# The gradient of one MLP weight moved to GpSimd at the turn of an attention block's training step, and three stores moved to the sync engine's queue

## Chip, cores and metric

The kernel runs on one core of one Trainium2 chip. The metric is the device time of one execution in microseconds; lower is better. Each kernel is timed several times, and its median is compared.

## What is computed

One decode step (one token, one batch) of a conditioned block, forward and backward in one launch. `c` is the condition, `w_mod` turns it into six modulation vectors; attention runs over a cache of 8192 keys and values for each of 32 heads of 192; the mixer behind it has an MLP of width 1536.

```python
mod = (_silu(c) @ w_mod).reshape(c.shape[0], 6, 1, -1)     # sa, ca, ga, sb, cb, gb
h = _layernorm(x) * (1 + ca) + sa
# _A_ref: q = h @ wq; p = softmax(q k^T / sqrt(192)); o = p v; o @ wo
x = x + ga * _A_ref(h, A_k_cache, A_v_cache, A_wq, A_wo)
h = _layernorm(x) * (1 + cb) + sb
# _B_ref at sequence length 1: the shifted half is zero, so
#   h + gelu(_layernorm(h) @ w3) @ w4
x = x + gb * _B_ref(h, B_w1, B_w2, B_w3, B_w4)
_out, _vjp = jax.vjp(_f, A_x, A_k_cache, A_v_cache, A_wq, A_wo, B_w3, B_w4, c, w_mod)
_grads = _vjp(grad_out)
```

The outputs are the result and nine gradients. The two large ones are those of the caches, dK and dV, 32 x 8192 x 192 in bfloat16 each (100 MB each). For one token each weight's gradient is an outer product of two vectors. The one that the change is about is dW4, the gradient of `B_w4` (1536 x 640): column `g` (the gelu's output, 1536) times row `dbo` (grad_out * gb, 640).

## The kernel before

**Forward (lines 493 to 591).** A loop over heads, two stages deep. Each head loads K and V in two tiles of 128 x 32 x 192 (1536 KB), on the queue of the sync engine (SP); DVE multiplies K by the broadcast q, TensorE sums, DVE and ScalarE (ACT) make the softmax, and TensorE accumulates K and V weighted by it.

**Turn (lines 592 to 778).** The MLP's forward and the start of the backward pass, on columns of 5 or 12 elements per partition. It is a serial chain between DVE and TensorE: two layernorms, `u` (L710 to 715), the gelu's parts, `du_bf` (L730), `g_f` (L732) and `g_bf` (L734), then `dn2` (L738), `dhb`, `dx1` and `dao_bf` (L742 to 755), and from it `do_bf` of the first pair of heads and its broadcast `do_pb` (L1044 to 1050).

**Backward (lines 1053 to 1099).** A loop over i = 0 to 31 with heads in falling order (`HS`: 31, 30, ...). For each head: `bwd_mult` multiplies both V tiles in place by `do_pb` on DVE, and TensorE sums them; `bwd_dv` makes dV for the next head, 20 of 32 columns of a tile on ACT (L877) and 12 on DVE (`pairs_outer`, L854), and stores it; `bwd_ds` and `bwd_dk` make dS and dK on DVE, and store dK. The dV of the first head, `HS[0]` = 31, is made ahead of the loop: its first tile all on DVE and stored in two halves of 768 KB, its second tile split as usual and stored in one of 1536 KB.

**Buffers.** dK and dV tiles come from the pool `big` (5 buffers). V tiles of the backward pass go round in six buffers of the pools `fv` and `bv`; `ring_load` issues a load as soon as the program has passed the place where an older tile was used up, and the load waits on the queue for that. Output tiles of the weight gradients come from the pool `bso`, tag "so", 2 buffers.

**Queues.** All loads of K, V and the weights in the loops go out from SP. All stores go out from GpSimd (POOL): `st2 = nc.gpsimd` (L675). POOL does nothing else after the constants at the start but to issue loads of `B_w3` and `B_w4` near the end of the forward pass. Each queue is served in the program's order; the orders of TensorE, DVE and ACT are pinned to the program's order by hand (`pin_order`), those of SP and POOL are what the program gives.

**Side jobs.** The outer products of the weights are spread over the backward loop by three lists, J0, J1, J2. `dbo_bc` (dbo broadcast to all partitions, 128 x 640 bfloat16) is made in the forward pass (L308), `g_f` at the turn; dW4 is made in four jobs, `job_dw4(k)`, at i = 17 to 20, each with three products of 128 x 640 on ACT (`tsc` with k = 0, L913) and one store of 480 KB. dW3 follows at i = 21 to 25, on DVE. dWo has gone ahead, at i = 1 to 16, and dWq and dWmod run from i = 9 on with loads, products and stores of their own.

Of the kernel before, what the change touches and what calls it, by code (L numbers as in the profile page):

```python
# [9 lines left out]
BF16 = mybir.dt.bfloat16  # L10
ALU = mybir.AluOpType
# [9 lines left out]
def kernel(  # L21
# [26 lines left out]
    nc = tc.nc  # L48
# [16 lines left out]
    P = 128  # L65
    D = A_x.shape[-1]
# [9 lines left out]
    NFC = F // P  # L76
    NMC = NMOD // P
    HH = HQ // 2
# [15 lines left out]
    def bank(tag, bufs=1, name=None, n=512):  # L94
        return psum[0].tile([P, n], FP32, tag=tag, name=name or "ps_" + tag, bufs=bufs)
# [31 lines left out]
    def ccol(n, name, dtype=FP32):  # L127
        return const.tile([P, n], dtype, name=name)
# [23 lines left out]
    def ln_cols(x_c, pfx, fill=lambda k: None):  # L152
        s1 = ccol(1, pfx + "_s1")
        nc.vector.reduce_sum(out=s1, in_=x_c, axis=AX.X)
        m_ps = neg_means(s1, 1, pfx + "_m")
        fill(0)
        xc = ccol(NDC, pfx + "_xc")
        add(xc, x_c, m_ps.to_broadcast([P, NDC]))
        sq = ccol(NDC, pfx + "_sq")
        s2 = ccol(1, pfx + "_s2")  # L160
        nc.vector.tensor_tensor_reduce(out=sq, in0=xc, in1=xc, scale=1.0 / D, scalar=0.0, op0=ALU.mult, op1=ALU.add, accum_out=s2)
        v_ps = col_sums(s2, 1, pfx + "_v")
        std = ccol(1, pfx + "_std")
        nc.scalar.activation(out=std, in_=v_ps, func=ACT.Sqrt, bias=eps_c[:, 0:1], scale=1.0)
        rstd = ccol(1, pfx + "_rstd")
        nc.vector.reciprocal(out=rstd, in_=std)
        fill(1)
        nrm = ccol(NDC, pfx + "_n")
        nc.vector.tensor_scalar(out=nrm, in0=xc, scalar1=rstd[:, 0:1], scalar2=None, op0=ALU.mult)
        return nrm, rstd  # L170
# [25 lines left out]
    def dve_copy(out, in_):  # L196
        nc.vector.tensor_copy(out=out, in_=in_)
# [11 lines left out]
    dV_hd = [out_3[0, h].rearrange("(p j) d -> p j d", p=P) for h in range(HQ)]  # L209
# [14 lines left out]
    def big_tile(name):  # L224
        return big.tile([P, JH, DH], BF16, name=name, tag="big")
# [44 lines left out]
    n0_c, r0 = ln_cols(x0_c, "ln0")  # L270
# [37 lines left out]
    dbo_bc = const.tile([P, D], BF16, name="dbo_bc")  # L308
# [214 lines left out]
    for i in range(1, HQ + 2):  # L523
        if i == HQ + 1:
            nc.scalar.activation(out=warm, in_=eps_c, func=ACT.Sqrt)
        c, p, pp = 2 <= i < HQ, 0 <= i - 1 < HQ, 0 <= i - 2 < HQ
# [75 lines left out]
    def w3T_some(n):  # L602
        for g in range(w3T_next[0], min(w3T_next[0] + n, NFC * NDC // 4)):
            t_ps = bank("s", 2, "t_ps", SB[0])
            for k in range(4):
                f, i = divmod(4 * g + k, NDC)
                nc.tensor.matmul(t_ps[:, k * P : (k + 1) * P], lhsT=w3n(i, f * P, (f + 1) * P), rhs=ident_bf, start=True, stop=True)
            k, r = divmod(g, NBT)
            nc.scalar.copy(out=w3T_t[k][:, r * 512 : (r + 1) * 512], in_=t_ps[:, 0:512])
        w3T_next[0] += n  # L610
# [30 lines left out]
    bso = ctx.enter_context(tc.tile_pool(name="bso", bufs=2, reuse_waits="tile"))  # L641
    bsm = ctx.enter_context(tc.tile_pool(name="bsmall", bufs=2, reuse_waits="tile"))
    HS = list(range(HQ - 1, -1, -1))
# [31 lines left out]
    st2 = nc.gpsimd  # L675
# [22 lines left out]
    n1_c, r1 = ln_cols(x1_c, "ln1", lambda k: w3T_some(k + 1))  # L698
# [32 lines left out]
    g_f = ccol(NFC, "g_f")  # L731
    mul(g_f, u, sg)  # L732
    g_bf = ccol(NFC, "g_bf", BF16)
    dve_copy(g_bf, g_f)  # L734
    dn2_ps = bank("b")
    for i in range(NDC):
        for f in range(NFC):
# [115 lines left out]
    def pairs_outer(o, pairs, vec, n):  # L853
        nc.vector.tensor_tensor(  # L854
            out=o.rearrange("p j (d r) -> p j d r", r=2),
            in0=pairs[:, :, None, :].to_broadcast([P, n, NP2, 2]),
            in1=vec.rearrange("p (d r) -> p d r", r=2)[:, None, :, :].to_broadcast([P, n, NP2, 2]),
            op=ALU.mult)

    def vec_of(d, h):  # L860
        return d[h // 2][:, (h % 2) * DH : (h % 2 + 1) * DH]
# [10 lines left out]
    def bwd_dv(h, t, na=NAV // 2, parts=1):  # L872
        o = big_tile("dV")
        j0 = t * JH
        doh = vec_of(do_pb, h)
        for jj in range(na):
            nc.scalar.activation(out=o[:, jj, :], in_=doh, func=ACT.Copy, scale=bst[h]["PF"][:, j0 + jj : j0 + jj + 1])  # L877
        n = JH // parts
        for r0 in range(0, JH, n):
            r1 = r0 + n  # L880
            ra = max(r0, na)
            pairs_outer(o[:, ra:r1, :], bst[h]["P2h"][:, j0 + ra : j0 + r1, :], doh, r1 - ra)
            st2.dma_start(out=dV_hd[h][:, j0 + r0 : j0 + r1, :], in_=o[:, r0:r1, :])  # L883

    def bwd_ds(h):
        dP = bsm.tile([P, J], FP32, name="dP")
# [24 lines left out]
    def tsc(out, in_, col, k):  # L911
        if k % 2 == 0:
            nc.scalar.activation(out=out, in_=in_, func=ACT.Copy, scale=col)  # L913
        else:
            nc.vector.tensor_scalar(out=out, in0=in_, scalar1=col, scalar2=None, op0=ALU.mult)

    def job_dw4(k):
        o = bso.tile([P, 3, D], BF16, name="dw4", tag="so")
        for cc in range(3):
            tsc(o[:, cc, :], dbo_bc, g_f[:, 3 * k + cc : 3 * k + cc + 1], 0)  # L920
        st2.dma_start(out=out_7[3 * k * P : 3 * (k + 1) * P, :].rearrange("(c p) r -> p c r", p=P), in_=o)

    def job_dw3(i):
        o = bso.tile([P, F], BF16, name="dw3", tag="so")
        tsc(o, du_bc, n2_c[:, i : i + 1], 1)
        st2.dma_start(out=out_6[i * P : (i + 1) * P, :], in_=o)

    def job_dwo(hp):
        o = bso.tile([P, 3, D], BF16, name="dwo", tag="so")
        for cc in range(3):  # L930
            tsc(o[:, cc, :], dao_bc, o_col_f[:, 3 * hp + cc : 3 * hp + cc + 1], 0)
        st2.dma_start(out=out_5[3 * hp * P : 3 * (hp + 1) * P, :].rearrange("(c p) r -> p c r", p=P), in_=o)
# [60 lines left out]
    J0, J1, J2 = [{i: [] for i in range(HQ)} for _ in range(3)]  # L993
    for k in range(HH):
        J1[1 + k].append(lambda hp=PS[k]: job_dwo(hp))
    for k in range(4):
        J1[1 + HH + k].append(lambda k=k: job_dw4(k))
    for k in range(NDC):
        J1[5 + HH + k].append(lambda i=k: job_dw3(i))

    def add_outer(at, name, view, lo, n, col_bf, rows_f, dram, acc, first):
        J2[at].append(lambda: job_outer_load(name, view, lo, n))
# [16 lines left out]
    for b, ks in enumerate(BATCHES):  # L1019
        units = [(PS[k], cc) for k in ks for cc in range(3)]  # L1020
        i = 1 + 2 * b
# [29 lines left out]
    bcast_dao()  # L1051
    mid_mm()
    bwd_dv(HS[0], 0, 0, 2)
    c_first = fin_c(PS[0], 1)
    bwd_dv(HS[0], 1)
    AHEAD = 2 * NPH
    for i in range(HQ):
        h, nxt = HS[i], HS[i + 1] if i + 1 < HQ else None
# [12 lines left out]
        if nxt is not None:  # L1071
            bwd_pf(nxt)
            for t in range(2):
                bwd_dv(nxt, t)
# [56 lines left out]
```

## Time and profile before

| | before |
|---|---|
| median of 3 runs | 1399.75 us (1398.21 to 1404.72) |
| profiled execution | 1395.47 us |
| its span, first to last instruction | 1393.7 us |
| busy: TensorE, DVE, ACT, POOL | 855.0, 1079.2, 964.8, 115.3 us |
| moved by DMA | 570.81 MB, mean 410 GB/s |
| SP's queue (q1) | 339.16 MB, 59.2% of 16 engines' span |
| POOL's queue (q0) | 229.85 MB, 39.2% |
| mean granted TensorE clock | 0.780 |

The profile is of one execution; times within it are counted in us from the first instruction. "Busy" leaves out the sequencers' own work: on SP everything is of that kind, on POOL the issue of a DMA is counted. The DMA share is the mean busy share of the core's 16 DMA engines, so 1 means that no transfer can be added; it comes out a little over 1 where packets overlap.

### The profile page before, as it was taken

The numbers are of one execution on the slowest core, as the hardware profiler recorded it, in microseconds if no ns is written. First come the engines' busy times: TensorE is split into PE (matmuls) and PEld (weight loads), VectorE is DVE, ScalarE is ACT, GpSimd is POOL, SyncE is SP. The second block draws the span as 40 slices with busy tenths as digits, with TensorE's granted clock in tenths as the row PEclk, the third lists the DMA queues.
The fourth block names the chain that finished last, engine by engine and source line by source line (L and its number), as shares of the span: only waits on it lengthen the run. The fifth ranks groups of instructions, "written<-read, shape, count | busy, mean of one in ns | idle before, by whom it ended". The sixth has DMA issues, their size and how long they took to land. (4 is left out here: it accounts for less than half of the span.)

```text
span 1393.7 us, 28111 instructions
## 1 busy us (share of the span) xinstructions
PE 855.0 (61%) x11519; PEld 672.3 (48%) x11519; DVE 1079.2 (77%) x1276; ACT 964.8 (69%) x2633; POOL 115.3 (8%) x207
## 2 busy tenths in 40 slices
PE   3699999999999999737644552434332344423242
PEld 3577777777777777626534451223222233212231
DVE  3678888888887886699996984966768669768697
ACT  1578777787787787794787396567666766566672
POOL 0000000000000000011101110211112111111011
PEclk9799999999999999666666566666676666766666
DMA  9999999999999999599999999999999999999998
GB/s 392 416 417 411 411 419 412 416 416 418 401 419 409 410 418 387 210 388 425 426 426 426 426 428 427 428 427 426 427 419 425 427 424 413 427 420 420 398 382 365
DMA packets 71711, 570.81 MB, mean 410 GB/s; under 512 B 6878, under 2 KB 18398, under 8 KB 31134
## 3 DMA queue, kind: packets, MB, share of 16 engines
q1 hardware_dynamic: 46496, 339.16, 59.2%
q0 software_dynamic: 25056, 229.85, 39.2%
q8 instruction: 90, 1.47, 0.4%
q14 instruction: 39, 0.32, 0.1%
q10 hardware_dynamic: 30, 0.00, 0.0%
HBM read 343.08 MB, written 225.91 MB: 408 GB/s over the span
## 5 line engine op out<-in xcount | busy, mean ns | idle before, releaser
L877 ACT ACTIVATE dV<-do_pb,PF 128x192 bf16<-128x192 bf16 x1260 | 439.5, 440 | 90.1 <-DMA out_dram<-dK 67.7
L869 PE MATMUL dP_ps<-V_sb,ident_bf 128*128 128x256 bf16 x1536 | 231.4, 326 | 264.8 <-DVE V_sb L131 264.8
L385 ACT ACTIVATE EK<-K_sb,E_f 128x192 bf16<-128x192 bf16 x1024 | 364.7, 442 | 22.8 <-PE kb_ps L426 15.2
L869 PEld LDWEIGHTS <-ident_bf 128*128 128x128 bf16 x1536 | 179.1, 117 | 317.4 <-issue 182.8
L854 DVE TENSOR_TENSOR dK<-dS,q_pb 128x6144 bf16<-128x6144 bf16 (+1 forms) x67 | 213.2, 3212 | 46.6 <-DMA out_dram<-dK 43.3
L131 DVE TENSOR_TENSOR prod<-K_sb,q_pb 128x6144 bf16<-128x6144 bf16 x64 | 214.7, 3354 | 22.0 <-DMA K_sb<-in_A_k_cache_dram 18.8
L131 DVE TENSOR_TENSOR V_sb<-V_sb,do_pb 128x6144 bf16<-128x6144 bf16 x64 | 211.8, 3351 | 2.6 <-DMA V_sb<-in_A_v_cache_dram 2.6
L410 PE MATMUL ps_a<-EK,V_sb 128*128 128x193 bf16 x2048 | 203.0, 252 | 4.7 <-DMA V_sb<-in_A_v_cache_dram 3.9
L410 PEld LDWEIGHTS <-V_sb 128*128 128x128 bf16 x2048 | 176.3, 100 | 23.8 <-issue 17.7
L854 DVE TENSOR_TENSOR dV<-P2h,do_pb 128x2304 bf16<-128x2304 bf16 (+1 forms) x65 | 87.3, 1369 | 57.7 <-DMA out_dram<-dV 53.1
L393 DVE TENSOR_TENSOR EK<-K_sb,P2h 128x1536 bf16<-128x1536 bf16 x128 | 121.7, 951 | 0.0
L418 PE MATMUL ps_b<-EK,V_sb 128*64 128x193 bf16 x2048 | 110.7, 250 | 8.1 <-DVE MB_all L134 8.0
L353 PE MATMUL S_ps<-prod,ident_bf 64*64 64x256 bf16 x3072 | 98.8, 276 | 6.7 <-DVE prod L131 6.7
L418 PEld LDWEIGHTS <-V_sb 128*64 128x64 bf16 x2048 | 84.1, 109 | 29.1 <-issue 28.8
L353 PEld LDWEIGHTS <-ident_bf 64*64 64x64 bf16 x3072 | 81.5, 109 | 22.4 <-issue 21.8
L374 ACT ACTIVATE E_f<-sm_ps,negm 128x64 f32<-128x64 f32 x32 | 10.1, 315 | 103.0 <-DVE negm L372 103.0
L883 POOL DMA_DIRECT2D out_dram<-dV x65 | 34.9, 537 | 447.1 <-ACT dV L877 272.5
L426 PE MATMUL kb_ps<-EK,hot_bf 128*32 128x384 bf16 x1024 | 65.7, 334 | 0.5 <-DVE q_bf L298 0.5
L194 ACT CAST do_pb<-bc_ps 128x384 bf16<-128x384 f32 x16 | 7.5, 470 | 70.4 <-PE bc_ps L190 70.4
L955 PEld LDWEIGHTS <-ident_bf 128*128 128x128 bf16 x112 | 14.3, 127 | 86.7 <-issue 83.3
L898 POOL DMA_DIRECT2D out_dram<-dK x67 | 37.2, 556 | 179.5 <-DVE dK L854 141.7
L391 DVE CAST EK<-E_f 128x16 bf16<-128x16 f32 x128 | 25.4, 199 | 33.5 <-PE kb_ps L426 27.3
(249 smaller groups left out, 816.1 us busy)
## 6 DMA issues: line engine op xcount, KB each, us to landing
V_sb<-in_A_v_cache_dram SPq DMA_DIRECT2D x126, 1536.0 KB, 11.7
K_sb<-in_A_k_cache_dram SPq DMA_DIRECT2D x64, 1536.0 KB, 9.5
out_dram<-dV POOLq DMA_DIRECT2D x63, 1536.0 KB, 19.8
out_dram<-dK POOLq DMA_DIRECT2D x63, 1536.0 KB, 21.3
wq<-in_A_wq_dram SPq DMA_DIRECT2D x3, 2560.0 KB, 34.0
wo_t<-in_A_wo_dram SPq DMA_DIRECT2D x16, 480.0 KB, 9.7
out_dram<-dwo POOLq DMA_DIRECT2D x16, 480.0 KB, 20.5
wq<-in_A_wq_dram SPq DMA_DIRECT2D x4, 1920.0 KB, 30.7
```

Of the source, the lines that this page charges most:

```text
L131: nc.vector.tensor_tensor(out=out, in0=a, in1=b, op=ALU.mult)
L353: nc.tensor.matmul(st["S_ps"][c0 : c0 + 64, r, t * JH : (t + 1) * JH, :], lhsT=ident_bf[64 * r : 64 * r + 64, 64 * r : 64 * r + 64], rhs=p ...
L385: nc.scalar.activation(out=EK[:, jj, 0:DH], in_=K_st[h, t][:, r * JQ + jj, :], func=ACT.Copy, scale=st["E_f"][:, j : j + 1])
L393: nc.vector.tensor_tensor(out=EK[:, NA:JQ, 0:DH].rearrange("p j (d r) -> p j d r", r=2), in0=K_st[h, t][:, r * JQ + NA : (r + 1) * JQ, :]. ...
L410: nc.tensor.matmul(st["A_ps"][:, 0 : DH + 1], lhsT=V_sb[:, r * JQ + jj, a0:a1], rhs=EK[:, jj, 0 : DH + 1], start=(q == 0 and jj == 0), sto ...
L418: nc.tensor.matmul(st["B_ps"][g : g + 64, 0 : DH + 1], lhsT=V_sb[:, r * JQ + jj, b0:b1], rhs=EK[:, jj, 0 : DH + 1], start=(q == 0 and jj < ...
L426: nc.tensor.matmul(kb_ps[g : g + 32, 0 : 2 * DH], lhsT=hot_bf[:, HQ - 1 - h : 2 * HQ - 1 - h], rhs=EK[:, jj : jj + 2, 0:DH], start=(h == 0 ...
L854: nc.vector.tensor_tensor(out=o.rearrange("p j (d r) -> p j d r", r=2), in0=pairs[:, :, None, :].to_broadcast([P, n, NP2, 2]), in1=vec.rea ...
L869: nc.tensor.matmul(bst[h]["dP_ps"][:, t * JH : (t + 1) * JH, :], lhsT=ident_bf, rhs=V_sb[:, :, k * DS : (k + 1) * DS], start=(k == 0), sto ...
L877: nc.scalar.activation(out=o[:, jj, :], in_=doh, func=ACT.Copy, scale=bst[h]["PF"][:, j0 + jj : j0 + jj + 1])
L883: st2.dma_start(out=dV_hd[h][:, j0 + r0 : j0 + r1, :], in_=o[:, r0:r1, :])
L898: st2.dma_start(out=dK_hd[h][:, j0 : j0 + n, :], in_=o[:, r0 : r0 + n, :])
```

## The change

dW4's twelve products of 128 x 640 are taken from ACT and from the backward loop. They are written right behind `g_f` and `g_bf`, on POOL (`nc.gpsimd.tensor_scalar`, `dbo_bc` times a column of `g_f`), in four tiles of the same pool, and POOL stores each tile there, in the same four stores of 480 KB. The job is gone from the lists, and the five jobs of dW3 move up from i = 21 to 25 to i = 17 to 21. The three stores of head 31's dV go out from SP's queue; those of the other heads stay on POOL's.

```diff
@@ -732,6 +732,11 @@
     mul(g_f, u, sg)
     g_bf = ccol(NFC, "g_bf", BF16)
     dve_copy(g_bf, g_f)
+    for k in range(NFC // 3):
+        o = bso.tile([P, 3, D], BF16, name="dw4", tag="so")
+        for cc in range(3):
+            nc.gpsimd.tensor_scalar(out=o[:, cc, :], in0=dbo_bc, scalar1=g_f[:, 3 * k + cc : 3 * k + cc + 1], scalar2=None, op0=ALU.mult)
+        nc.gpsimd.dma_start(out=out_7[3 * k * P : 3 * (k + 1) * P, :].rearrange("(c p) r -> p c r", p=P), in_=o)
     dn2_ps = bank("b")
@@ -880,7 +885,7 @@
             pairs_outer(o[:, ra:r1, :], bst[h]["P2h"][:, j0 + ra : j0 + r1, :], doh, r1 - ra)
-            st2.dma_start(out=dV_hd[h][:, j0 + r0 : j0 + r1, :], in_=o[:, r0:r1, :])
+            (nc.sync if h == HS[0] else st2).dma_start(out=dV_hd[h][:, j0 + r0 : j0 + r1, :], in_=o[:, r0:r1, :])
@@ -914,12 +919,6 @@
-    def job_dw4(k):
-        o = bso.tile([P, 3, D], BF16, name="dw4", tag="so")
-        for cc in range(3):
-            tsc(o[:, cc, :], dbo_bc, g_f[:, 3 * k + cc : 3 * k + cc + 1], 0)
-        st2.dma_start(out=out_7[3 * k * P : 3 * (k + 1) * P, :].rearrange("(c p) r -> p c r", p=P), in_=o)
-
@@ -993,10 +992,8 @@
-    for k in range(4):
-        J1[1 + HH + k].append(lambda k=k: job_dw4(k))
     for k in range(NDC):
-        J1[5 + HH + k].append(lambda i=k: job_dw3(i))
+        J1[1 + HH + k].append(lambda i=k: job_dw3(i))
```

## The prediction, made before the result

> **What bounds the kernel now.** I read the page's slices first, to see where the transfers have room, then the table of windows around the turn, then the timeline there, then the groups of what is moved, then the waits of the stage that loses work.
>
> Of the slices, two rows matter:
>
> ```profile
> DMA  9999999999999999599999999999999999999998
> GB/s 392 416 417 411 411 419 412 416 416 418 401 419 409 410 418 387 210 388 425 426 426 426 426 428 427 428 427 426 427 419 425 427 424 413 427 420 420 398 382 365
> ```
>
> The DMA engines are full but for one slice, the seventeenth (557 to 592 us): the turn from forward to backward. Windows of 4 us there, and longer ones later (columns: length, then busy us of PE, PEld, DVE, ACT, POOL, granted clock, DMA share, GB/s):
>
> ```profile
> 572.00:576.00 4.00, 3.92 (x79) 3.54 (x76) 0.92 (x8) 1.91 (x4) 0.00 (x0) 0.50 0.48 200
> 576.00:580.00 4.00, 2.78 (x33) 2.27 (x32) 1.96 (x13) 2.35 (x6) 0.00 (x0) 0.50 0.01 4
> 580.00:584.00 4.00, 3.86 (x73) 3.65 (x70) 3.51 (x3) 4.00 (x12) 0.56 (x1) 0.50 0.10 43
> 584.00:588.00 4.00, 1.23 (x11) 1.04 (x11) 3.94 (x5) 4.00 (x13) 0.56 (x1) 0.50 0.87 350
> 588.00:592.00 4.00, 2.84 (x14) 2.03 (x14) 4.00 (x2) 3.97 (x13) 0.53 (x1) 0.50 0.70 295
> 592.00:596.00 4.00, 4.00 (x36) 3.41 (x34) 3.97 (x8) 4.00 (x13) 0.35 (x1) 0.92 0.62 184
> ...
> 600.00:740.00 140.00, 80.78 (x498) 68.50 (x498) 134.65 (x172) 104.60 (x280) 19.29 (x33) 0.65 1.01 426
> 1040.00:1130.00 90.00, 35.05 (x207) 24.35 (x205) 65.53 (x50) 65.17 (x159) 15.88 (x27) 0.67 1.01 424
> ```
>
> From 572 to 596 the DMA engines idle 4 x (0.52 + 0.99 + 0.90 + 0.13 + 0.30 + 0.38) = 12.9 us; POOL computes nothing. From 600 on the transfers are the limit (share 1.01), and DVE nearly is up to 740 (134.65 of 140). The timeline of the turn:
>
> ```profile
> 571.83 0.16 DVE L131 TENSOR_TENSOR g_f<-u,sg 128x12 f32<-128x12 f32 x1
> ...
> 576.18 0.23 DVE L140 SCALAR_TENSOR_TENSOR dhb<-lb_t,ln_rstd,dbo_c 128x5 f32<-128x5 f32 x1
> ...
> 580.48 3.43 DVE L854 TENSOR_TENSOR dV<-P2h,do_pb 128x3072 bf16<-128x3072 bf16 x2 [1.11 <-ACT do_pb L194]
> ...
> 582.54 0.56 POOL L883 DMA_DIRECT2D out_dram<-dV  x1 [42.75 <-DVE dV L854]
> ...
> 588.35 0.53 POOL L883 DMA_DIRECT2D out_dram<-dV  x1 [3.59 <-ACT PF L685]
> ...
> 593.64 0.33 SPq L322 DMA_DIRECT2D V_sb<-in_A_v_cache_dram  x1
> ...
> 595.64 0.53 POOL L883 DMA_DIRECT2D out_dram<-dV  x1 [6.76 <-ACT dV L877]
> ```
>
> g_f is there at 572.0. From then to 580.48 a serial chain of small DVE and PE steps (dhb, dx1, dao_bf, do_bf, do_pb) makes the first dV possible; nothing useful can be stored until it ends. That chain is the hole.
>
> **Part 1: what leaves the full stage.** dW4 today:
>
> ```profile
> L913 ACT ACTIVATE dw<-dbo_bc,g_f x12: 811/812/817, 1044.7 to 1126.3; 128x640 bf16<-128x640 bf16 x12
> L921 POOL DMA_DIRECT2D out_dram<-dw x4: 765/765/765, 1047.2 to 1127.4; - x4
> ```
>
> Four stores of 480 KB are 1.97 MB; at the 424 GB/s of 1040:1130 that is 4.6 us of transfer. Does all of it reach the end? Between 1040 and 1344 the longest waits of DVE and ACT on transfers are for output buffers (dV L854 on the landing of dV 47.6 us, dV L877 on dK 38.0), and the chain that ended last runs through DMA until 1343.42, then through DVE with hardly a gap. So that last stretch starts 4.6 earlier: -4.6. The ACT time (12 x 0.81 = 9.8 us) is worth nothing by itself: ACT is busy 65.17 of 90 there and idles for buffers. The five dW3 jobs move four heads forward, into the heads that lose dW4: DVE 5 x 0.61 us, stores 5 x 0.55 us of POOL's queue, bytes unchanged. DVE is busy 65.53 of 90 there, so 0; without that cover 3.1 us.
>
> **Part 2: what enters the turn, on POOL.** No row shows a tensor_scalar on POOL. Its rows that compute are at the start: a 128x128 affine select, which reads, computes and writes, 0.284 us; a 128x128 memset, which only writes, 0.206; a 128x1 memset, 0.100. Scaled linearly from 128 to 640 elements: 0.100 + 639 x (0.184 / 127) = 1.03 us by the first, 0.62 by the second. The first is nearer in kind: 1.03. Two "so" buffers, 0.77 us for each issue, and 3.8 us to landing (the two dV stores of 768 KB here): first tile 572.0 to 575.1, issued by 575.9; second to 579.0, issued by 579.7; third (first landed 578.9) to 582.8, issued by 583.6; fourth to 586.7, issued by 587.5. All four stores have idle DMA ahead of 596, and POOL's next job, the store of the second head's dV, comes at 595.64: 8.1 us of cover. If that is gone, that store and the dK stores behind it in POOL's queue wait.
>
> **Part 3: what POOL's arithmetic does to DVE.** The trace has none of the one beside the other's two-operand work, so the price lies between nothing and the full length of every POOL instruction; below nothing is excluded, since no step of the chain is shortened. Beside the chain (574.74 to 578.41, eight small two-operand DVE steps) lie the last instruction of the first tile and three of the second: 0 to 4 x 1.03 = 4.1 us on the way to 580.48, and the whole backward half moves with that. Met at a random point, half of an instruction is left: I take 2.1. Beside the big products after 580.48 lie the other six: 0 to 6.2 us on DVE, 3.1 by the same half. The two V loads at 593.64 and 596.26 wait for the products of V by do_pb on DVE and the sums on PE; when they are late the DMA engines, already at 0.62, idle until the dV store at 595.64, which waits for ACT: 0 to 2.0, I take 1.0. After that a cushion covers it: at 614.05, when the next V load is issued, a dK store is outstanding until 620.5, and at 637.91 stores are until 641.4. So 3.5 us of DVE lateness are free; beyond them each us costs a us, as DVE has no slack to 740.
>
> **Part 4: dV of head 31 on SP's queue.** Its three stores pass behind the V load issued at 564.93 (landed 576.28) and ahead of those at 593.64 and 596.26. SP waits in order for each dV; the last is ready at 588.3, so the load keeps 5.3 us of cover. No store on SP is in the trace; as to landing, the load of 593.64 took 7.28 us for 1536 KB and the dV store of 588.35 on POOL 7.66. Taken as 0; bounds -0.7 (three issues, 0.33 against 0.56 us) and, only if a dV is late by over 5.3 us more than the load, the excess.
>
> **Sum.** -4.6 + 2.1 + 1.0 = -1.5 us. The profiled execution took 1395.47 us (span 1393.7, 1.8 around it), so 1394.0 for it; it lies 4.3 under the median 1399.75, so by the median 1398.3.
>
> **Rivals.** *B, no disturbance*: POOL and DVE pass each other by, and -4.6 is left: 1395.1, 1394.4 with SP's 0.7. For it: the chain's DVE steps last 0.17 us with gaps of up to 2.27 between them. Against it: after 580.48 DVE has no gaps.
>
> *C, slower*: DVE and POOL shut each other out wholly. Each of ten POOL instructions then holds up DVE for its whole length, and POOL waits for a product of 1.35 to 3.35 us each time, so it comes free at about 604 rather than 587 and the second head's dV store is late by some 8 us, about as late as DVE's own work. Price 10 x 1.03 - 4.6 = +5.7: 1405.5. The point from which it decides: slower than now from 0.46 us per instruction, by over 0.5% (7.0 us) from 1.16, which the 1.03 is near; at 1.3 it is +8.4, 1408.2. For it: from 580.48 to 740 nearly every DVE instruction has two operands in SBUF, and there is no slack to give it back. Against it: part falls where transfers have other work.
>
> The Trainium skill, page "SBUF — State Buffer", section "Who interferes with whom", says just this: a VectorE instruction with two SBUF inputs contends with a GpSimd instruction that reads SBUF, and the one that starts first blocks the other for the whole instruction. By that rule the time would be between my sum and C, depending on who starts first; no run here shows it yet.
>
> *D, it doesn't do what it says*: the first tiles wait, for their place in the freed forward pools or for a landing, until the engines are full from 600 on. Then bytes only move inside the full stage: 0, 1399.75. Against it: the forward pools' last reader (PE L426) ran at 564.
>
> **Numbers.** My sum 0.47, B 0.22, C 0.26, D 0.05. A measurement of this kernel can tell about 0.5% from no change, 7 us. No case gains that by its sum (most 5.3), so faster gets 0.08 for scatter and for what I don't see. Most of C lies above 7 us if an instruction takes over 1.16: 0.17, and 0.03 from the others: slower 0.20, same 0.72. Low end: B with SP's 0.7, and 1.5 for the runs (the lowest is that far under the median): 1392.9. High end: C at 1.3 us: 1408.2.
>
> **What would show it.** TENSOR_SCALAR rows on POOL at L738 or near, 12 of about 1.0 us from 572; DMA share well above 0.01 and 0.10 in 576:584; the first dV product at about 582.6 instead of 580.5 (B: 580.5; C: 584.6); POOL free before 596 (C: after 600); DMA share from 600 still 1.01, and from 1130 on everything earlier by the same few us. I am wrong if a POOL instruction takes far over 1.03, if the first dV comes over 4 us late, or if the DMA share after 600 drops below 1.

## The result: slower, 1409.3 us against 1399.1

Six runs of the changed kernel have a median of 1409.3 us (1406.53 to 1413.35), six of the kernel before 1399.08; the estimated ratio of the two is 1.0056 (95% interval 1.0033 to 1.0078), 4.6 to 10.9 us more; the quotient of the two medians alone, 1.0073, lies inside that interval. All ratios below are to the kernel before, run on the same chip. Run again later beside other kernels (e9 below), it was 1.0041 (1.0022 to 1.0060). The prediction, 1398.3 in 1392.9 to 1408.2, was wrong: the time is above its range, and the change moved it clearly.

One caution for reading the profiles. The forward pass is the same program in nearly all kernels here, yet `g_f` comes at 571.8 us in the profile of before, 576.2 in that of the changed kernel and 573.9 in that of its repeat. So I compare times behind `g_f`, within one profile, and take the ratios for the times.

The slices of the changed kernel:

```profile
DMA  9999999999999999679999999999999999999998
GB/s 393 400 410 407 409 418 413 418 419 401 416 410 406 416 413 372 239 268 422 426 428 425 427 427 427 428 427 428 426 426 416 426 422 405 427 420 426 423 383 362
```

The hole was one slice wide and is now two: it has been filled a little (239 GB/s instead of 210) and has grown by the slice behind it (268 instead of 388). The windows of 4 us show which part is new (columns as in the prediction):

```profile
576.00:580.00 4.00, 3.91 (x77) 3.50 (x77) 0.94 (x9) 2.13 (x5) 3.40 (x2) 0.50 0.69 289
580.00:584.00 4.00, 2.35 (x27) 1.92 (x26) 3.01 (x14) 2.46 (x6) 4.00 (x3) 0.50 0.02 4
584.00:588.00 4.00, 3.60 (x82) 3.36 (x79) 2.76 (x4) 2.95 (x9) 3.96 (x4) 0.50 0.34 123
...
604.00:608.00 4.00, 0.90 (x5) 0.77 (x6) 3.79 (x11) 3.81 (x11) 3.96 (x3) 0.56 1.03 363
608.00:612.00 4.00, 0.48 (x3) 0.32 (x3) 4.00 (x2) 3.40 (x10) 4.00 (x2) 0.50 0.44 181
612.00:616.00 4.00, 0.00 (x0) 0.00 (x0) 4.00 (x3) 4.00 (x13) 3.97 (x1) 0.50 0.00 0
616.00:620.00 4.00, 1.86 (x9) 1.28 (x9) 4.00 (x2) 0.34 (x1) 2.96 (x5) 0.50 0.59 221
```

Between 608 and 620 the DMA engines idle for 4 x (0.56 + 1.00 + 0.41) = 7.9 of 12 us while DVE and POOL are busy throughout, or nearly, and ACT until 616: finished output lies in SBUF and nobody sends it. POOL's own rows, from the groups of dW4's tile (ns shortest/median/longest) and from the timeline:

```profile
L738 POOL TENSOR_SCALAR dw<-dbo_bc,g_f x12: 1872/1898/7410, 576.6 to 608.6; 128x640 bf16<-128x640 bf16 x12
```

```profile
576.60 1.89 POOL L738 TENSOR_SCALAR dw<-dbo_bc,g_f 128x640 bf16<-128x640 bf16 x1 [32.35 <-DVE g_bf L197]
...
608.56 7.41 POOL L738 TENSOR_SCALAR dw<-dbo_bc,g_f 128x640 bf16<-128x640 bf16 x1
616.26 0.81 POOL L739 DMA_DIRECT2D out_dram<-dw  x1 [0.30 <-POOL dw L738]
617.08 1.11 POOL L888 DMA_DIRECT2D out_dram<-dV  x2
618.17 1.05 POOL L903 DMA_DIRECT2D out_dram<-dK  x2
```

An instruction takes 1.87 to 1.89 us where DVE has only small steps, and up to 7.41 beside DVE's products. All twelve together take 36.3 us, 13.7 more than 12 x 1.88, and POOL comes free at 617.1, 40.9 us behind `g_f`. Then four stores go out in a row: two of dV and two of dK. The first of these dV tiles had been ready for 16.3 us: ACT had done its columns at 600.4, and DVE ended its own at 600.7:

```profile
599.38 1.36 DVE L859 TENSOR_TENSOR dV<-P2h,do_pb 128x2304 bf16<-128x2304 bf16 x1
```

That is the second hole.

### The profile page after: what moved, and what is told of

Read it like the earlier page. It is cut to its first block, busy times and chain, and to the rows that moved or that the text cites. A ratio compares the mean times of both kernels' runs of the same rounds, so it can differ in the third digit from the quotient of the medians.

```text
span 1404.9 us, 28114 instructions
## 1 busy us (share of the span) xinstructions
PE 869.2 (62%) x11519; PEld 682.3 (49%) x11519; DVE 1083.9 (77%) x1276; ACT 956.3 (68%) x2621; POOL 149.3 (11%) x216
## 4 chain that ended last, share of the span: by engine, by line
DMA 47%; DVE 23%; PE 14%; issue 9%; POOL 4%; ACT 3%; another core or an unknown queue 1%; POOLq 0%; ACTq 0%; DVEq 0%; SPq 0%
DMA out_dram<-dK 14%; DMA out_dram<-dV 14%; DMA K_sb<-in_A_k_cache_dram 11%; DVE prod L131 7%; PE ps_a L410 5%; DVE dK L859 3%; DMA V_sb<-in_A_v_cache_dram 3%; PE ps_b L418 3%; DVE V_sb L131 3%; POOL dw L738 3%; DVE S L357 2%; DMA out_dram<-wq_o 2%; DVE EK L393 2%; PE S_ps L353 2%; DMA out_dram<-dwo 2%
## 5 line engine op out<-in xcount | busy, mean ns | idle before, releaser
L874 PE MATMUL dP_ps<-V_sb,ident_bf 128*128 128x256 bf16 x1536 | 237.4, 331 | 257.0 <-DVE V_sb L131 257.0
```

The costliest lines, as they stand in the source:

```text
L874: nc.tensor.matmul(bst[h]["dP_ps"][:, t * JH : (t + 1) * JH, :], lhsT=ident_bf, rhs=V_sb[:, :, k * DS : (k + 1) * DS], start=(k == 0), sto ...
```

## Experiments

Two theories. **Q**: the loss is POOL's queue; its arithmetic ends late and finished stores stand behind it. **D**: the loss is DVE's, held up by POOL's reads. The number that ties the trace to the time is the idle DMA in the 48 us behind `g_f`. These are windows of just that length, of before and of the changed kernel (DMA share next to last):

```profile
571.83:619.83 48.00, 27.17 (x294) 22.24 (x292) 42.04 (x67) 43.59 (x120) 4.85 (x9) 0.64 0.73 294
```

```profile
576.21:624.21 48.00, 26.19 (x287) 21.73 (x286) 41.77 (x56) 35.48 (x99) 42.14 (x21) 0.60 0.62 239
```

Idle is 48 x (1 - 0.73) = 13.0 us before and 18.2 after, 5.3 more although 4.6 us of transfers were added.

**e1: head 31's dV from SP alone.**

```diff
-            st2.dma_start(out=dV_hd[h]...
+            (nc.sync if h == HS[0] else st2).dma_start(out=dV_hd[h]...
```

> Only the dV stores of head 31 go from SP; dW4 stays in the loop on ACT. Theory Q (the loss is POOL's queue: its products end 40 us after g_f and four stores wait behind them): no change, 0 within 2 us, DMA idle in the 48 us behind g_f as before, 12.6 to 12.9 us. Rival S (stores on SP hold up the V loads): 4 to 8 us slower, and the V loads of head 30 issued later than 22 us behind g_f.

Measured: 0.9999 (0.9977 to 1.0020), share 0.73 in the 48 us. This half of the change costs and brings nothing that shows, within 3 us.

**e2: dW4 on POOL alone**, all dV stores on `st2`.

> Only dW4 goes to POOL at the turn; all dV stores stay on POOL, so head 31's three wait behind dW4 too, in the program's order. Theory Q: slower than the changed kernel, since head 31's dV, ready 11 to 17 us behind g_f, now also waits for POOL until some 40 us: DMA idle behind g_f 4 to 10 us above the changed kernel's 18, so 10 to 20 us slower than before. Rival D (the loss is DVE's own lateness, 3.8 us up to the first dK, beside POOL's reads): as the changed kernel, 6 to 10 us slower than before.

Measured: 1.0041 (1.0023 to 1.0059), 3 to 8 us; share 0.59, idle 19.7. So dW4 on POOL carries the whole loss, but Q's 10 to 20 us was a miss: POOL's queue did not keep the order in which the program names these stores, which the description of the kernel before takes for granted; why is not known. The first two of head 31's dV stores went out between dW4's tiles, and only the third, at 613.78, behind the last:

```profile
605.41 0.61 POOL L888 DMA_DIRECT2D out_dram<-dV  x1
606.02 0.79 POOL L739 DMA_DIRECT2D out_dram<-dw  x1
...
612.40 0.61 POOL L888 DMA_DIRECT2D out_dram<-dV  x1
```

By its time alone e2 doesn't tell Q from D; e3 does.

**e3: the queue opened.** POOL computes as in the changed kernel; the stores that would stand behind it go from SP.

```diff
-            (nc.sync if h == HS[0] else st2).dma_start(out=dV_hd[h]...
+            (nc.sync if h in HS[0:3] else st2).dma_start(out=dV_hd[h]...
-            st2.dma_start(out=dK_hd[h]...
+            (nc.sync if h in HS[0:2] else st2).dma_start(out=dK_hd[h]...
```

> The changed kernel, and also the stores of dV of heads 30 and 29 and of dK of heads 31 and 30 go from SP, so nothing but dW4's own stores waits behind POOL's products. Theory Q: the second idle stretch (5.6 us in the 36 to 48 us behind g_f) is gone, DMA idle in 48 us below 13 us, and the kernel is within 3 us of before. Rival D: DVE is as late as in the changed kernel (first dK 31.5 us behind g_f against 27.7) and the kernel stays 6 us or more slower than before.

Measured: 1.0004 (0.9980 to 1.0027); idle 10.6 us (share 0.78):

```profile
577.45:625.45 48.00, 26.09 (x288) 21.78 (x287) 42.40 (x57) 42.70 (x119) 39.45 (x16) 0.60 0.78 309
```

POOL is as late as in the changed kernel, its last dW4 store at 617.5 or 40 us behind `g_f`, and so is DVE, its first dK 31.5 us behind it; the third V load goes out 46.3 us behind `g_f` (46.4 in the changed kernel). But the second hole is gone and the loss with it. Q holds, and D falls as the reason why the kernel is slower than before. The gain of 4.6 us doesn't come back, though. Two of dW4's four stores go out only 27.8 and 40.1 us behind `g_f`, where the engines of the kernel before are full again (share 0.99 from 24 us on), and DVE's 3.8 us of lateness remain; no run separates the two. (The profiled execution of e3 was the slowest of its ten, so only its first stretch is read here.)

**e4: the same work at the same place on DVE.** The six products of the first two tiles while TensorE makes `dn2`, the others in the next gaps of the chain; stores on POOL.

```diff
-            nc.gpsimd.tensor_scalar(out=o[:, cc, :], in0=dbo_bc, scalar1=g_f[...
+    dw4_some(0, 6)      # behind g_bf: nc.vector.tensor_scalar(...), POOL stores each full tile
+        dw4_some(6, 7)  # in lb1_fill
+    dw4_some(7, 8)      # behind bwd_pf_dve(HS[0])
+    dw4_some(8, 11)     # behind do_bf
+    dw4_some(11, 12)    # behind the first dV
```

> dW4 at the turn, but on DVE in the gaps of its chain: six products while TensorE makes dn2 (gap 2.27 us), one behind lb1's sums, one behind P2h, three behind do_bf, one behind the first dV; stores on POOL; dV on POOL. The dW3 rows (128x1536 in 0.61 us) give about 0.35 us for each of 640. Theory Q (the idea of filling the hole is right, the engine wrong): the first dV is under 1 us later behind g_f than the 8.65 us of before, DMA idle behind g_f falls by 3 to 4.6 us, and the kernel is 2 to 4.6 us faster than before. Rival N (bytes taken from the full stage are given back elsewhere): idle falls but the time stays within 1 us of before.

Measured: 0.9958 (0.9931 to 0.9985), 2 to 10 us faster. From its timeline, and its 48 us:

```profile
574.86 1.86 DVE L742 TENSOR_SCALAR dw<-dbo_bc,g_f 128x640 bf16<-128x640 bf16 x6
...
583.51 3.43 DVE L868 TENSOR_TENSOR dV<-P2h,do_pb 128x3072 bf16<-128x3072 bf16 x2
```

```profile
574.58:622.58 48.00, 26.79 (x294) 22.01 (x292) 45.08 (x79) 43.32 (x120) 8.01 (x13) 0.64 0.85 336
```

Six products on DVE take 1.86 us together, what one takes on POOL. The first dV comes 8.93 us behind `g_f` (8.65 before), and idle falls from 13.0 to 7.2.

**e5: POOL writes but reads nothing.**

```diff
-            nc.gpsimd.tensor_scalar(out=o[:, cc, :], in0=dbo_bc, ...
+            for _ in range(3):
+                nc.gpsimd.memset(o[:, cc, :], 0.0)
```

> The changed kernel with each of POOL's twelve products replaced by three memsets of the same tile (they write and read nothing; dW4's values are left out): about as much work by length, no reads. Theory R (POOL's reads wait while a DVE instruction with two operands in SBUF runs, and come in only where one without them stands): the memsets keep one length throughout, beside V products too, POOL comes free before 26 us behind g_f, the first dK is at 27.5 to 28.5 us behind g_f, and the kernel is 2 to 5 us faster than before. Rival A (any work of POOL waits for DVE): memsets beside the V products take several us as the products did, POOL is free only after 35 us, and the kernel is 5 to 9 us slower.

Measured: 1.0000 (0.9985 to 1.0016). On lengths R was right: 36 memsets of 0.62 to 0.65 us, beside DVE's dV products too, POOL free 13.6 us behind `g_f`, first dK 28.0 behind it. The time was a miss, for a reason the run shows: without `g_f` to wait for, the memsets began ahead of it, and a small DVE step of the chain waited for them:

```profile
577.12 4.22 DVE L724 TENSOR_SCALAR sg<-sg 128x12 f32<-128x12 f32 x1 [0.40 <-ACT sg L719]
```

In the kernel before it takes 0.17 us. It ended when POOL paused for a buffer (memsets 577.80 to 581.31, the next at 582.75). Why it did not come in earlier, while POOL issued a store (577.04 to 577.80), is not shown.

**e6: half the dose.** Tiles 0 and 1 on POOL at the turn, tiles 2 and 3 in the loop on ACT (`range(2)` in place of `range(NFC // 3)`, `job_dw4` kept for k = 2, 3).

> Half the dose: two of dW4's four tiles on POOL at the turn, two stay in the loop on ACT. Theory Q: six products end some 15 us behind g_f, ahead of the second head's first dV store (23.8 us in the profile of before), so no store waits for POOL; 2.3 us of transfers leave the full stage, the chain loses 0.7: 0 to 2.5 us faster than before, DMA idle in 48 us 10 to 12 us. Rival P (half the loss for half the work): 3 to 4 us slower than before.

Measured: 0.9985 (0.9965 to 1.0005), share 0.75. POOL is free 15.6 us behind `g_f`, and the second head's store goes out when its data are ready, with POOL idle ahead of it:

```profile
594.21 0.82 POOL L739 DMA_DIRECT2D out_dram<-dw  x1 [0.30 <-POOL dw L738]
603.97 0.57 POOL L888 DMA_DIRECT2D out_dram<-dV  x1 [8.94 <-ACT dV L882]
```

Half the work doesn't bring half the loss but none: the cost begins where POOL is late for a store. P falls.

**e7: POOL's lengths by themselves**, in the forward pass.

```diff
+    for rep in range(6):
+        for n in (128, 320, 640):
+            nc.gpsimd.tensor_scalar(out=scr[:, 0:n], in0=dbo_bc[:, 0:n], scalar1=ca1[:, 0:1], ...
+        nc.gpsimd.memset(scr, 0.0)
+        nc.gpsimd.tensor_copy(out=scr, in_=dbo_bc)
```

> The kernel before with extra work on POOL in the forward pass, its results unused: six times a tensor_scalar of 128, 320 and 640 columns, a memset and a copy of 640. It gives POOL's lengths by themselves. If length goes by the element, as my prediction scaled it, the three sizes give a line through about 0.1 us at no column; from the changed kernel's 1.88 us at 640 that means 0.46 at 128 and 0.99 at 320. Theory R: the shortest of each size are on that line, and those that meet a K product on DVE (3.35 us) are up to 3 us longer; the memsets are not. Rival O (a fixed cost of over 1 us for each instruction): the line meets 0 columns above 1 us.

The first three have DVE idle; the others run beside it:

```profile
18.05 0.61 POOL L313 TENSOR_SCALAR E_all<-dbo_bc,ca 128x128 bf16<-128x128 bf16 x1 [16.39 <-ACT dbo_bc L194]
18.75 1.08 POOL L313 TENSOR_SCALAR E_all<-dbo_bc,ca 128x320 bf16<-128x320 bf16 x1
19.93 1.88 POOL L313 TENSOR_SCALAR E_all<-dbo_bc,ca 128x640 bf16<-128x640 bf16 x1
...
27.20 0.63 POOL L314 MEMSET E_all<- 128x640 bf16 x1
...
30.39 3.59 POOL L313 TENSOR_SCALAR E_all<-dbo_bc,ca 128x128 bf16<-128x128 bf16 x1
...
34.07 4.14 POOL L313 TENSOR_SCALAR E_all<-dbo_bc,ca 128x320 bf16<-128x320 bf16 x1
```

```profile
26.36 3.36 DVE L131 TENSOR_TENSOR prod<-K_sb,q_pb 128x6144 bf16<-128x6144 bf16 x1 [1.23 <-DMA K_sb<-in_A_k_cache_dram]
30.11 3.40 DVE L131 TENSOR_TENSOR prod<-K_sb,q_pb 128x6144 bf16<-128x6144 bf16 x1 [0.39 <-DMA K_sb<-in_A_k_cache_dram]
33.90 3.36 DVE L131 TENSOR_TENSOR prod<-K_sb,q_pb 128x6144 bf16<-128x6144 bf16 x1 [0.40 <-DMA K_sb<-in_A_k_cache_dram]
```

From 128 to 640 columns 1.27 us more: 2.5 ns a column and 0.29 us fixed; O falls. The two that meet a K product take 3.0 us longer than their own length and end less than one own length behind it; the memset of 27.20, inside a product, keeps its 0.63. That settles the first half of R: POOL's reads wait for such a DVE instruction, its writes don't. The second half, that POOL comes in only where a DVE instruction without two operands stands, doesn't hold everywhere (last section).

**e8 and e9: the version to keep, and the changed kernel again.** e8 is the whole change with DVE in POOL's place (e4, and head 31's dV from SP); e9 is the changed kernel as it stands.

> The whole change with one thing exchanged: dW4's products on DVE in the gaps, as in e4, and head 31's dV stored from SP. Theory Q: as e4, 3 to 8 us faster than before, DMA idle in the 48 us behind g_f 6.5 to 8 us. Rival N: within 2 us of before, e4's gain having been scatter.

> The changed kernel itself, beside e8 on one chip. Theory Q: 5 to 10 us slower than before; POOL comes free about 40 us behind g_f again, DMA idle in those 48 us about 18 us. If the loss hung on this one execution's late forward pass instead, it would be within 3 us of before.

Measured: e8 0.9951 (0.9932 to 0.9970), 1396.4 against 1402.4 us for the kernel before on that chip, idle 8.2 us (share 0.83); e9 1.0041, idle 18.2 (share 0.62), POOL free 40.9 us behind `g_f`. e4 and e8 beat both kernels, by some 6 and 7 us over before. So e9 is 12.6 us behind e8 by these ratios. Opening the queue (e3) gains 5 to 7 us over the changed kernel; the remainder, about half, is what the products cost more on POOL than on DVE even with the queue open.

Idle DMA and time together (idle from the shares of the 48 us, against 13.0 of before):

| | idle, us | change of the time, us (interval) |
|---|---|---|
| changed kernel, e9 | +5.3, +5.3 | +7.8 (4.6 to 10.9), +5.7 (3.1 to 8.4) |
| e2, dW4 on POOL alone | +6.7 | +5.7 (3.2 to 8.3) |
| e1, SP alone | 0 | -0.1 (-3.2 to 2.8) |
| e3, queue opened | -2.4 | +0.6 (-2.8 to 3.8) |
| e5, memsets (their hold-up ahead of `g_f` not counted) | -1.4 | 0.0 (-2.1 to 2.2) |
| e6, half | -1.0 | -2.1 (-4.9 to 0.7) |
| e4, e8, on DVE | -5.8, -4.8 | -5.9 (-9.7 to -2.1), -6.9 (-9.5 to -4.2) |

In every row the idle DMA of the turn, read from one execution, lies inside the interval of the time. The bytes are the same in all of them.

## Why the prediction was wrong, step by step

- **Part 1, bytes into the hole (-4.6): right as an idea, not had by this kernel.** In the changed kernel two of the four stores came too late for the hole, at 604.0 and 616.3 (27.8 and 40.1 us behind `g_f`). e4 and e8 get the gain: 4.8 to 5.8 us less idle, and 6 to 7 less in time with intervals that hold 4.6. Rival N fell.
- **Part 2, length on POOL (1.03 us): mis-sized, 1.88.** I scaled a 128-column affine select; its slope per column was 1.45 ns, the tensor_scalar's is 2.5. Over twelve instructions this alone put POOL's end 10.2 us later, past the 8.1 of cover that I had named. The same scaling of the memset rows gives 0.63 (I wrote 0.62), and a memset of 640 columns did take 0.63 in e7: the scaling held within one operation and failed from one to another.
- **Part 3: the step that failed.** I priced the meeting of POOL and DVE wholly on DVE's side, and let POOL run through at its bare length. DVE lost little, and within what I had taken: the first dV came 0.70 us late behind `g_f` (I took 2.1) and 3.1 more went by up to the first dK (I took 3.1); the V loads were 0.95 us late. POOL lost 13.7 us in waiting, which was in no term of the sum; only rival C named it. 25.4 us later than my plan (10.2 and 13.7, and 1.5 in issues and small gaps), it stood in front of four finished stores.
- **The cover.** I wrote what hides POOL's work and what it costs when that is gone ("that store and the dK stores behind it wait"), but put no price on it in the sum. That wait was the loss: the 7.9 us of idle engines from 608 to 620, which e3 removes. Of the three signs of being wrong that I had named, two came: an instruction far over 1.03, and a DMA share under 1 behind 600.
- **Part 4, SP: right**, 0 within 3 us (e1).
- **Rival C** had the sign and nearly the size (+5.7), and by a side remark the cause: POOL free late, the second head's store late. That its size came near is luck: its price was ten full lengths on DVE, which didn't come. Ten DVE instructions were longer than in the kernel before, each by 0.21 to 0.69 us. POOL was free 40.9 us behind `g_f` where C's plan had 32. The rule of the Trainium skill that stood beside C (page "SBUF — State Buffer", section "Who interferes with whom") agrees with the runs in both halves: POOL's reads wait for DVE's two-operand products (3.59 instead of 0.61 us in e7), and POOL's writes alone do not (memset 0.63). That the first one blocks the other for its whole instruction is not what DVE's rows show (last section). B and D didn't happen.

I gave "slower by over 0.5%" 0.20; the error behind that was the same: a chance for DVE being held up, none for a queue being held up.

## What to carry to other kernels

An engine that issues the stores is a server for everyone who has output; before giving it arithmetic, add up its bare lengths and its waits, and compare the end with the next store it owes. When two engines may shut each other out, price both sides: here the one with back-to-back work gave up 4 us and the other 14. And an idle stretch of the transfers is worth filling if the work can be done before it ends: one product cost 0.31 us in DVE's gaps and 1.88 on POOL.

## What the runs showed of the hardware

POOL doesn't get its turn after each DVE product. Its last instruction began at 608.56, waited through both products of dK, and ended 1.75 us behind the start of the short copy out of PSUM that followed them:

```profile
607.67 6.63 DVE L859 TENSOR_TENSOR dK<-dS,q_pb 128x6144 bf16<-128x6144 bf16 x2
614.22 0.15 DVE L197 COPY c_bc<-c_ps 128x2 f32<-128x2 f32 x1
```

Between two V products (594.65) another did come in, and the second product took 3.95 us instead of 3.35. So both orders occur; why it was shut out between dK's two products was not tried.

DVE, in turn, was not seen to wait for the whole of a POOL product. The cast below is the DVE instruction that the changed kernel lengthened most, from 0.17 to 0.86 us, beside POOL instructions of 1.88; in e2 the same cast took 1.09. And in e7 a K product that began 1.1 us into such an instruction (26.36 against 25.26) kept its 3.36. What POOL does in the rest of its 1.88 us isn't shown.

```profile
604.79 0.86 DVE L197 CAST do_bf<-dof 128x3 bf16<-128x3 f32 x1
```

On POOL a tensor_scalar with a column of scalars costs 2.5 ns a column, but a plain copy of 640 columns 0.72 us in all and a memset 0.63: lengths of one operation there say little of another. And a stream of memsets held up a one-operand DVE step of 128x12 for 4.22 us (e5), which fits the rule for tensor_scalar and casts on DVE in their two-port modes in the same section of the Trainium skill's page "SBUF — State Buffer".
